# Regrouping the weight loads and moving the x transposes in a fused attention and maxout kernel on one Trainium2 core

## The chip, the core and the metric

The kernel runs on one core of a Trainium2 chip. Its engines are TensorE (PE, matmuls and transposes by matmul), VectorE (DVE), ScalarE (ACT), GpSimd (POOL) and SyncE (SP, which here only issues DMAs). The metric is the time of one execution on the device in microseconds (us); lower is better. Times of a kernel are given as the median of several runs. A single further execution is profiled, and all durations of rows come from that one.

## The reference

There are two stages. The first is a small attention in both directions between x (batch 8, heads 8, 512 positions, 64 wide) and 32 state vectors for each batch and head; the second is a feed-forward layer that takes the largest of three products.

```python
def _attn_ref(x, state):
    scale = 1.0 / np.sqrt(D)
    a  = softmax(scale * x @ state.T)          # per batch and head: 512 x 32
    xread = a @ state
    a2 = softmax(scale * state @ x.T)          # 32 x 512
    sread = a2 @ x
    return np.concatenate([xread, sread], axis=2)

def _moe_ref(x, w1, w2, w3, w_out):            # x: 4352 x 512, w: 512 x 768
    h = np.maximum(np.maximum(x @ w1, x @ w2), x @ w3)
    return h @ w_out                           # 768 x 512
```

The rows of the second stage are, for each batch, 512 rows of `xread` and 32 of `sread`, the heads side by side. (Softmax is written short here; the reference subtracts the maximum and divides by the sum.)

## The kernel before

The kernel is one program written out in program order under a manual schedule: every engine runs its instructions in the order in which the Python code emits them, and semaphores hold an instruction until its inputs and its buffer are there. Buffers come from pools that hand out a fixed number per tag in rotation, so an instruction that takes a buffer also waits until the last reader of that buffer's earlier tile has finished. In PSUM there are four buffers of tag `pw`[...] and two of tag `two`.

`xread` is never formed. Since `xread` is `a @ state` and the layer multiplies it by W, the kernel multiplies the states of a batch with W first (`g_cols`, giving G) and then a with G (`x_maxout`). W has 768 columns in six slices of 128, numbered m = 0 to 5; slice m of w1, w2 and w3 is needed together. For one batch b the steps are:

- `x_transpose(b, g, copy)`, on PE, or `x_transpose_dma(b)`, a DMA transpose issued by SP: x of the batch to `xT`. Batches 0, 1 and 2 use PE, 3 to 7 the DMA.
- `scores(b, g0, g1)`: PE multiplies `xT` with a block-diagonal arrangement of the states (`bd`; one tile `bds[k]` serves batches 2k and 2k+1), ACT takes the exponential to `e`.
- `softmax(b, g0, g1, mul)`: DVE sums and inverts, and `mul` (POOL or DVE) writes the product a.
- `a_transpose(b, g, copy)` on PE, or `a_transpose_dma(b)` by SP: a to `aT`.
- `g_cols(b, ms, copies, defer)`: eight small matmuls for each slice m of `ms`, then a copy of the slice of G out of PSUM by the engine named (ACT unless told otherwise), put off into the next maxout where `defer` says so.
- `x_maxout(b, m)`: six matmuls, ACT copies the first product (`t0`), DVE takes the two maxima and writes `ht`.
- `ffn_out(b, j)`: six matmuls of `ht` with `wout_sb`, a copy by ACT, and after every second j a store by POOL.
- `sread(b)`: the other direction, 32 small matmuls, two DVE instructions, and a DMA transpose by SP into `ats`, which is put on a list and issued by `late_transposes`.

`states(k, copy)` makes `bds[k]`: for k = 0 and 1 with PE transposes, for k = 2 and 3 with a DMA transpose by SP into `stT` and two POOL copies.

All loads that change the type from float32 to bfloat16 (W, x, w_out) are issued by POOL, in program order with POOL's own arithmetic. `load_x(b)` brings one batch of x, `load_st(k, eng)` the states of two batches, `load_w(c, parts)` one chunk of W by three DMAs. The chunks are slices 0, 1, 2-3 and 4-5. Half of x of batch 0 is loaded by SP in float32 and cast by DVE, so that the start doesn't wait for POOL. `keep_busy(n)` runs n matmuls on zeros whose result nobody reads.

The code has three parts: the loads and preparations; the start, written out by hand (from the first `keep_busy(5)`, line 329, to the loop), where the attention of batches 0, 1 and 2 is laid between the first slices of maxout; and the main loop over b = 2 to 7. In the loop each `x_maxout(b, m)` is followed by the list `slots[m]`, which holds the attention of batch n = b + 1, the missing slices of G, and `ffn_out(b - 1, j)`. The order within a slot is that in which the lists were filled.

Of the kernel before, what the change touches and what calls it, by code (L numbers as in the profile page):

```python
# [15 lines left out]
def kernel(  # L16
# [14 lines left out]
    nc = tc.nc  # L31

    B, H, S, D = x.shape
# [11 lines left out]
    XW = H * J * D  # L45
# [11 lines left out]
    def load_st(k, eng):  # L57
        eng.dma_start(
            out=st_f[k],
            in_=state[2 * k:2 * k + 2].rearrange("b h n d -> (b h n) d").rearrange("(p t) d -> p t d", t=4))  # L60
# [8 lines left out]
    def load_x(b):  # L69
        nc.gpsimd.dma_start(  # L70
            out=x_sb[b][:, 0:XW].rearrange("p (h jd) -> p h jd", h=H),
            in_=x[b].rearrange("h (p j) d -> p h (j d)", j=J))
# [9 lines left out]
    ident = const.tile([128, 128], BF16, name="ident")  # L82
    make_identity(nc, ident)
    nc.gpsimd.dma_start(out=x0_sb[1], in_=x0_heads(1))
    load_x(1)

    chunks = ((0, 1), (1, 2), (2, 4), (4, 6))
    w_sb = [wpool.tile([128, HS, 3, (m1 - m0) * 128], BF16, name=f"w{m0}") for m0, m1 in chunks]
    wout_sb = wpool.tile([128, NM, d_model], BF16, name="wout")

    def load_w(c, parts=(0, 1, 2)):
        m0, m1 = chunks[c]
        for i in parts:
            w = (moe_w1, moe_w2, moe_w3)[i]
            nc.gpsimd.dma_start(  # L95
                out=w_sb[c][:, :, i, :],
                in_=w.rearrange("(kk p) f -> p kk f", p=128)[:, :, m0 * 128:m1 * 128])
# [4 lines left out]
        return w_sb[c], slice(f, f + 128)  # L102

    load_w(0)
    for b in range(B):
        nc.gpsimd.memset(x_sb[b][:, XW:XW + D], 1.0)
    load_w(1, (0,))
    bds = [data.tile([128, 2, H, 2, Ns], BF16, name=f"bd{k}") for k in range(B // 2)]
    nc.vector.memset(bds[0], 0.0)

# [4 lines left out]
    def keep_busy(n):  # L115
        p = pp.tile([128, 1024], F32, tag="two", name="idle")
        for _ in range(n):
            nc.tensor.matmul(p[:, 0:512], zero[:, 0:128], zero, start=True, stop=True)  # L118
# [7 lines left out]
    def states_cast(k, cast):  # L126
        cast(out=st[k], in_=st_f[k].unsqueeze(2).to_broadcast((128, 4, 2, D)))
# [16 lines left out]
    xT, e, a, aT, G, ht, osb = {}, {}, {}, {}, {}, {}, {}  # L144

    def new(d, b, shape, name, bufs=2):
        d[b] = work.tile(shape, BF16, tag=name, bufs=bufs, name=name)

    def x_transpose(b, g, copy):

        if g == 0:
            new(xT, b, [128, H, 2, 128], "xT")
        p = pp.tile([128, HS, 2, 128], BF16, tag="pw", bufs=4, name="pxt")
        for s in range(HS):
            for jj in range(2):
                nc.tensor.transpose(
                    p[:, s, jj, :],
                    xv[b][:, 2 * s + g, 2 * jj:2 * jj + 2, :].rearrange("p j d -> p (j d)"), ident)
        copy(out=xT[b].rearrange("p (s g) j t -> p g s j t", g=2)[:, g], in_=p)  # L159

    def x_transpose_dma(b):
        new(xT, b, [128, H, 2, 128], "xT")
        nc.sync.dma_start_transpose(out=xT[b].rearrange("p h j t -> p (h j) t"), in_=x_sb[b][:, 0:XW])

    def scores(b, g0, g1):
        n = g1 - g0
        if g0 == 0:
            new(e, b, [128, J, 2, HS, Ns], "e")
        if n == 2:
            p = pp.tile([128, J, n, HS, Ns], F32, tag="two", name="ps")  # L170
        else:
            p = pp.tile([128, J, n, HS, Ns], F32, tag="pw", bufs=4, name="psh")
        for jj in range(2):
            for g in range(g0, g1):
                for s in range(HS):
                    h = 2 * s + g
                    nc.tensor.matmul(  # L177
                        p[:, 2 * jj:2 * jj + 2, g - g0, s, :], xT[b][:, h, jj, :],
                        bd(b, h).rearrange("p c n -> p (c n)"),
                        start=(g == g0 and s == 0 and (n == 2 or jj == 0)),  # L180
                        stop=(g == g1 - 1 and s == HS - 1), skip_group_check=True)
        nc.scalar.activation(out=e[b][:, :, g0:g1], in_=p, func=AF.Exp, scale=scale)  # L182

    def softmax(b, g0, g1, mul):
        n = g1 - g0
        if g0 == 0:
            new(a, b, [128, J, 2, HS, Ns], "a")
        den = work.tile([128, J, n, HS], F32, tag=f"den{n}", name="den")
        nc.vector.reduce_sum(out=den, in_=e[b][:, :, g0:g1], axis=AX.X)  # L189
        rden = work.tile([128, J, n, HS], F32, tag=f"rden{n}", name="rden")  # L190
        nc.vector.reciprocal(out=rden, in_=den)  # L191
        mul(  # L192
            out=a[b][:, :, g0:g1].rearrange("p j g s n -> p j (g s) n"),
            in0=e[b][:, :, g0:g1].rearrange("p j g s n -> p j (g s) n"),
            in1=rden.rearrange("p j g s -> p j (g s)").unsqueeze(3).to_broadcast((128, J, n * HS, Ns)))

    def a_transpose(b, g, copy):

        if g == 0:
            new(aT, b, [128, J, 2, 128], "aT", bufs=3)  # L200
        p = pp.tile([128, J, 128], BF16, tag="pw", bufs=4, name="pat")
        for j in range(J):
            nc.tensor.transpose(p[:, j, :], a[b][:, j, g].rearrange("p s n -> p (s n)"), ident)
        copy(out=aT[b][:, :, g, :], in_=p)
# [76 lines left out]
    def x_maxout(b, m):  # L281
        maxout(b, m, 512,
               lambda i, k: G[b][:, k, m * 384 + i * 128:m * 384 + i * 128 + 128],
               lambda k: aT[b][:, :, k, :], 2)
# [40 lines left out]
    def late_transposes():  # L325
        while late:
            late.pop(0)()
# [8 lines left out]
    x_transpose(0, 0, dve)  # L336
    x_transpose(0, 1, dve)
    scores(0, 0, 1)
    softmax(0, 0, 1, nc.gpsimd.tensor_mul)
    load_w(1, (1, 2))  # L340
    scores(0, 1, 2)
    softmax(0, 1, 2, nc.vector.tensor_mul)
    keep_busy(4)
    x_transpose(1, 0, act)
    x_transpose(1, 1, dve)
    a_transpose(0, 0, act)
    a_transpose(0, 1, dve)
    g_cols(0, (0,), (dve,))
    scores(1, 0, 1)
    scores(1, 1, 2)  # L350
    load_w(2)
    softmax(1, 0, 1, nc.gpsimd.tensor_mul)
    load_w(3, (0,))
    softmax(1, 1, 2, nc.gpsimd.tensor_mul)
    load_w(3, (1, 2))
    load_st(1, nc.gpsimd)
    load_x(2)
    x_maxout(0, 0)
    g_cols(0, (1,))
    g_cols(1, (0,))  # L360
    sread(0)
    x_maxout(0, 1)
    nc.gpsimd.dma_start(out=wout_sb, in_=moe_w_out.rearrange("(kk p) f -> p kk f", p=128))
    for k in range(2, B // 2):
        load_st(k, nc.gpsimd)
    load_x(3)
    sread(1)
    a_transpose(1, 0, act)
    a_transpose(1, 1, dve)
    g_cols(0, (2, 3), defer=(False, True))  # L370
    x_maxout(1, 0)
    x_maxout(0, 2)
    g_cols(1, (1, 2), defer=(False, True))
    x_maxout(0, 3)
    states_cast(1, pool)
    g_cols(0, (4, 5), defer=(False, True))
    x_maxout(1, 1)
    states(1, act)
    x_transpose(2, 0, dve)
    x_transpose(2, 1, act)  # L380
    x_maxout(0, 4)
    g_cols(1, (3, 4), defer=(False, True))
    x_maxout(1, 2)
    scores(2, 0, 2)
    x_maxout(0, 5)
    g_cols(1, (5,))
    x_maxout(1, 3)
    softmax(2, 0, 2, nc.gpsimd.tensor_mul)
    late_transposes()
    x_transpose_dma(3)  # L390
# [1 line left out]
    x_maxout(1, 4)  # L392
    g_cols(2, (0, 1))
    ffn_out(0, 1)
    load_x(4)
    for k in range(2, B // 2):
        states_cast(k, pool)
    x_maxout(1, 5)
# [3 lines left out]
    ffn_out(0, 2)  # L402
    ffn_out(0, 3)
    late_transposes()


    for b in range(2, B):
        n = b + 1
        slots = [[] for _ in range(NM)]
        if n < B:  # L410
            if n + 1 < B:
                slots[0].append(lambda: x_transpose_dma(n + 1))
            slots[0].append(lambda: scores(n, 0, 2))
            slots[1].append(lambda: softmax(n, 0, 2, nc.gpsimd.tensor_mul))
            slots[2].append(lambda: a_transpose_dma(n))
            if n % 2 and n + 1 < B:
                slots[2].append(lambda: states((n + 1) // 2, pool))
            slots[5].append(late_transposes)
            if n + 2 < B:
                slots[0].append(lambda: load_x(n + 2))  # L420
        else:
            for m in range(NM):
                slots[m].append(lambda m=m: s_maxout(m))
        slots[1].append(lambda: g_cols(b, (2, 3)))
        slots[2].append(lambda: g_cols(b, (4, 5)))
        if n < B:
            slots[3].append(lambda: sread(n))
            slots[4].append(lambda: g_cols(n, (0, 1), defer=(False, True)))
        for j, m in enumerate((1, 2, 4, 5)):
            slots[m].insert(0 if m > 2 else len(slots[m]), lambda j=j: ffn_out(b - 1, j))  # L430
        for m in range(NM):
            x_maxout(b, m)
            for f in slots[m]:
                f()
# [36 lines left out]
```

## Time and profile before

| what | value |
|---|---|
| median of 5 runs | 160.56 us (160.24 to 161.56) |
| the profiled execution, own time | 161.74 us |
| its span (first to last instruction) | 160.0 us |
| PE busy | 149.5 us (93%) |
| ACT busy, DVE busy, POOL busy | 96.8, 94.6, 51.0 us |
| DMA moved | 21.72 MB, mean 136 GB/s |
| DMA transposes of x: issue on SP, min, median, max | 1.33, 3.18, 6.46 us |
| DMA transposes of x: to landing, min, median, max | 4.3, 5.0, 9.1 us |
| DMA transposes of the states (`stT`): to landing | 2.5 and 3.5 us |

Times in the profile are microseconds from the start of the span. In the page's second part the span is cut into 40 equal slices of 4 us, and a digit is a busy share in tenths; PEclk is the clock that PE was granted, in tenths. A line of the chain of waits has the start, the length and the engine with its line number. A line of the timeline has start, length, engine, line, operation, the tile written and the tile read, and in brackets the idle time before and what ended it. A line of the waits has the total, the number and the longest. "PEq" and "SPq" are the sequencers of PE and SP; a DMA's row on SPq or POOL is the time of issuing it, not that of the transfer.

### The profile page before, as it was taken

Reading aid. Unit: us, or ns where it says so; the run is one execution under the profiler, and the core shown is the slowest. Engines: PE = TensorE matmul, PEld = TensorE weight load, DVE = VectorE, ACT = ScalarE, POOL = GpSimd, SP = SyncE. Lnnn points to the kernel's source line nnn. Section 1 sums busy time; section 2 is a strip of 40 time slices with the busy share of each in tenths; the row PEclk is TensorE's granted clock in tenths of the full one; section 3 lists DMA queues with packets and bytes.
Section 4 is the critical chain, followed back from the end, with each engine's and each line's share of the span. In section 5 each row is a group of like instructions: output and inputs, shape, how many; then the busy total and the mean of one; then the engine's idle time right before and its main releaser. Section 6 shows DMA issues by size and latency. Waiting matters only on the chain.

```text
span 160.0 us, 3568 instructions
## 1 busy us (share of the span) xinstructions
PE 149.5 (93%) x1432; PEld 70.7 (44%) x1432; DVE 94.6 (59%) x161; ACT 96.8 (61%) x156; POOL 51.0 (32%) x72
## 2 busy tenths in 40 slices
PE   6775799999999999999999999999999999999990
PEld 2442353544454444444444444444434465466550
DVE  4788358668545864577367736673767384475200
ACT  3364548995737837783778287828782737633340
POOL 8859981000553404541034061410051100100150
PEclk9999779999999999999999999999999999999999
DMA  3999999998079997999969967070307030030365
GB/s 117 207 164 119 189 195 177 234 135 133 0 159 242 137 141 130 277 165 170 201 171 118 101 124 280 4 205 2 135 0 205 0 137 0 0 131 4 131 220 173
DMA packets 36720, 21.72 MB, mean 136 GB/s; under 512 B 21952, under 2 KB 34368, under 8 KB 36704
## 3 DMA queue, kind: packets, MB, share of 16 engines
q0 software_dynamic: 17216, 15.08, 49.8%
q1 hardware_dynamic: 19344, 6.29, 23.0%
q8 instruction: 11, 0.18, 0.4%
q10 hardware_dynamic: 144, 0.13, 0.2%
q14 instruction: 5, 0.04, 0.1%
HBM read 15.20 MB, written 8.91 MB: 151 GB/s over the span
## 4 chain that ended last, share of the span: by engine, by line
PE 83%; DMA 6%; DVE 4%; ACT 3%; POOL 1%; issue 1%; SPq 0%; DVEq 0%; POOLq 0%
PE pw L271 42%; PE po L308 28%; PE pg L250 7%; DMA w<-in_moe_w_dram 3%; PE psr L222 3%; DMA x0f<-in_x_dram 2%; PE ps L177 2%; DVE t L278 1%; ACT t L275 1%; ACT G L256 1%; DVE ht L279 1%; PE ph L300 1%; POOL a L192 1%; DVE x L335 1%; POOL w L95 0%
## 5 line engine op out<-in xcount | busy, mean ns | idle before, releaser
L271 PE MATMUL pw<-aT,G 128*128 128x512 bf16 x288 | 71.3, 385 | 0.9 <-DVE G L256 0.5
L278 DVE TENSOR_TENSOR t<-t,pw 128x512 bf16<-128x512 bf16 (+1 forms) x54 | 35.1, 649 | 42.9 <-ACT t L275 27.1
L308 PE MATMUL po<-wout,ht 128*128 128x512 bf16 x198 | 47.4, 380 | 0.2 <-DVE ht L279 0.2
L256 ACT CAST G<-pg 128x768 bf16<-128x768 f32 x47 | 36.3, 806 | 8.3 <-PE pg L250 7.9
L271 PEld LDWEIGHTS <-G 128*128 128x128 bf16 x288 | 26.6, 98 | 33.0 <-issue 3.9
L279 DVE TENSOR_TENSOR ht<-t,pw 128x512 bf16<-128x512 bf16 (+1 forms) x54 | 35.5, 658 | 5.6
L275 ACT CAST t<-pw 128x512 bf16<-128x512 f32 (+1 forms) x54 | 30.6, 566 | 13.0 <-PE pw L271 12.3
L311 ACT COPY osb<-po 128x512 f32<-128x512 f32 x33 | 19.3, 586 | 23.6 <-PE po L308 23.2
L308 PEld LDWEIGHTS <-ht 128*128 128x128 bf16 x198 | 17.8, 98 | 24.7 <-issue 4.5
L192 POOL TENSOR_TENSOR a<-e,rden 128x1024 bf16<-128x1024 bf16 (+1 forms) x9 | 14.6, 1621 | 40.0 <-DVE rden L191 30.6
L320 POOL DMA_DIRECT2D out_dram<-osb x14 | 7.9, 566 | 46.5 <-ACT osb L311 36.7
L250 PE MATMUL pg<-w,bd 64*32 64x384 bf16 x384 | 12.8, 328 | 2.5 <-DMA w<-in_moe_w_dram 2.2
L189 DVE TENSOR_REDUCE den<-e 128x32 f32<-128x1024 bf16 (+1 forms) x10 | 9.9, 991 | 0.5 <-ACT e L182 0.5
L95 POOL DMA_DIRECT2D w<-in_moe_w_dram x12 | 9.1, 774 | 0.0
L250 PEld LDWEIGHTS <-bd 64*32 64x32 bf16 x384 | 3.6, 89 | 12.4 <-issue 11.8
L271 PE MATMUL pw<-ats,w 128*128 128x256 bf16 x72 | 8.8, 273 | 0.0
L182 ACT ACTIVATE e<-ps 128x1024 bf16<-128x1024 f32 x6 | 6.1, 1024 | 3.8 <-PE ps L177 3.7
L271 PEld LDWEIGHTS <-w 128*128 128x128 bf16 x72 | 7.1, 98 | 2.1
L140 POOL COPY bd<-stT 64x512 bf16<-64x512 bf16 x4 | 4.3, 1071 | 10.8 <-DMA stT<-st 10.7
L70 POOL DMA_DIRECT2D x<-in_x_dram x7 | 6.5, 923 | 0.0
L118 PE MATMUL idle<-zero 128*128 128x512 bf16 x14 | 4.9, 492 | 1.2 <-DVE zero L81 1.2
L177 PEld LDWEIGHTS <-xT 128*128 128x128 bf16 x128 | 4.7, 98 | 2.4 <-DVE xT L159 0.8
(45 smaller groups left out, 66.3 us busy)
## 6 DMA issues: line engine op xcount, KB each, us to landing
out_dram<-osb POOLq DMA_DIRECT2D x14, 512.0 KB, 3.7
x<-in_x_dram POOLq DMA_DIRECT2D x7, 512.0 KB, 9.2
w<-in_moe_w_dram POOLq DMA_DIRECT2D x6, 256.0 KB, 6.0
w<-in_moe_w_dram POOLq DMA_DIRECT2D x6, 128.0 KB, 6.8
wout<-in_moe_w_out_dram POOLq DMA_DIRECT2D x1, 768.0 KB, 11.7
x0f<-in_x_dram SPq DMA_DIRECT2D x1, 512.0 KB, 4.0
out_dram<-osb SPq DMA_DIRECT2D x1, 512.0 KB, 2.7
stf<-in_state_dram POOLq DMA_DIRECT2D x3, 128.0 KB, 11.0
```

Of the source, the lines that this page charges most:

```text
L95: nc.gpsimd.dma_start(out=w_sb[c][:, :, i, :], in_=w.rearrange("(kk p) f -> p kk f", p=128)[:, :, m0 * 128:m1 * 128])
L177: nc.tensor.matmul(p[:, 2 * jj:2 * jj + 2, g - g0, s, :], xT[b][:, h, jj, :], bd(b, h).rearrange("p c n -> p (c n)"), start=(g == g0 and s ...
L189: nc.vector.reduce_sum(out=den, in_=e[b][:, :, g0:g1], axis=AX.X)
L192: mul(out=a[b][:, :, g0:g1].rearrange("p j g s n -> p j (g s) n"), in0=e[b][:, :, g0:g1].rearrange("p j g s n -> p j (g s) n"), in1=rden.r ...
L250: nc.tensor.matmul(p[32 * s:32 * s + 32, g, 0:384].rearrange("p (i f) -> p i f", i=3), bd(b, 2 * s + g)[64 * g:64 * g + 64, g, :], w[64 * ...
L256: copy(out=G[b][:, :, m * 384:(m + 1) * 384], in_=p[:, :, 0:384])
L271: nc.tensor.matmul(p[:, 0:n], lhs(i, k), rhs(k), start=(k == 0), stop=(k == nk - 1))
L275: nc.scalar.copy(out=t0[:, 0:n], in_=pw[0][:, 0:n])
L278: nc.vector.tensor_max(t1[:, 0:n], t0[:, 0:n], pw[1][:, 0:n])
L279: nc.vector.tensor_max(ht[b][:, m, :], t1[:, 0:n], pw[2][:, 0:n])
L308: nc.tensor.matmul(p, ht[b][:, m, j * 128:(j + 1) * 128], wout_sb[:, m, :], start=(m == 0), stop=(m == NM - 1))
L311: act(out=o[:, j, :], in_=p)
```

## The change

- W is cut into three chunks of two slices each instead of four (1, 1, 2, 2). `load_w` always loads all three matrices of a chunk. The first chunk is issued ahead of x of batch 1, the second ahead of batch 0's first product on POOL, the third behind it.
- The start is reordered: slices of `g_cols` and `x_maxout` of batch 0 come ahead of and between the steps of batch 1's attention. Some copies go to other engines (`g_cols(0, (1,))` and slice 3 to DVE, the second `a_transpose(1, ...)` to ACT). `sread(0)` and `sread(1)` come later.
- Of the eight memsets that write the column of ones behind x, two stay at the top and six move behind the loads.
- x is loaded one batch further ahead (`load_x(4)` in the start, then `n + 3` in the loop).
- `xT` gets three buffers instead of two. The DMA transpose of batch n + 2 is issued in slot 2, behind that of a(n), where before that of batch n + 1 was issued in slot 0; that of batch 4 is issued ahead of the loop.

```diff
-    load_x(1)
-
-    chunks = ((0, 1), (1, 2), (2, 4), (4, 6))
+
+    chunks = ((0, 2), (2, 4), (4, 6))
...
-    def load_w(c, parts=(0, 1, 2)):
+    def load_w(c):
         m0, m1 = chunks[c]
-        for i in parts:
-            w = (moe_w1, moe_w2, moe_w3)[i]
+        for i, w in enumerate((moe_w1, moe_w2, moe_w3)):
...
     load_w(0)
-    for b in range(B):
+    load_x(1)
+    for b in range(2):
         nc.gpsimd.memset(x_sb[b][:, XW:XW + D], 1.0)
-    load_w(1, (0,))
...
-            new(xT, b, [128, H, 2, 128], "xT")
+            new(xT, b, [128, H, 2, 128], "xT", bufs=3)
...
     def x_transpose_dma(b):
-        new(xT, b, [128, H, 2, 128], "xT")
+        new(xT, b, [128, H, 2, 128], "xT", bufs=3)
...
     scores(0, 0, 1)
+    load_w(1)
     softmax(0, 0, 1, nc.gpsimd.tensor_mul)
-    load_w(1, (1, 2))
     scores(0, 1, 2)
     softmax(0, 1, 2, nc.vector.tensor_mul)
-    keep_busy(4)
+    keep_busy(5)
+    g_cols(0, (0,))
+    a_transpose(0, 0, act)
+    a_transpose(0, 1, dve)
+    g_cols(0, (1,), (dve,))
+    load_w(2)
+    load_st(1, nc.gpsimd)
+    x_maxout(0, 0)
     x_transpose(1, 0, act)
     x_transpose(1, 1, dve)
-    a_transpose(0, 0, act)
-    a_transpose(0, 1, dve)
-    g_cols(0, (0,), (dve,))
+    x_maxout(0, 1)
     scores(1, 0, 1)
     scores(1, 1, 2)
-    load_w(2)
     softmax(1, 0, 1, nc.gpsimd.tensor_mul)
-    load_w(3, (0,))
     softmax(1, 1, 2, nc.gpsimd.tensor_mul)
-    load_w(3, (1, 2))
-    load_st(1, nc.gpsimd)
     load_x(2)
-    x_maxout(0, 0)
-    g_cols(0, (1,))
-    g_cols(1, (0,))
-    sread(0)
-    x_maxout(0, 1)
     nc.gpsimd.dma_start(out=wout_sb, in_=moe_w_out.rearrange("(kk p) f -> p kk f", p=128))
     for k in range(2, B // 2):
         load_st(k, nc.gpsimd)
     load_x(3)
-    sread(1)
+    load_x(4)
+    for b in range(2, B):
+        nc.gpsimd.memset(x_sb[b][:, XW:XW + D], 1.0)
+    g_cols(0, (2, 3), (act, dve))
+    sread(0)
+    g_cols(1, (0,))
+    x_maxout(0, 2)
     a_transpose(1, 0, act)
-    a_transpose(1, 1, dve)
-    g_cols(0, (2, 3), defer=(False, True))
+    a_transpose(1, 1, act)
+    g_cols(1, (1,))
+    x_maxout(0, 3)
     x_maxout(1, 0)
-    x_maxout(0, 2)
-    g_cols(1, (1, 2), defer=(False, True))
-    x_maxout(0, 3)
-    states_cast(1, pool)
     g_cols(0, (4, 5), defer=(False, True))
     x_maxout(1, 1)
+    states_cast(1, pool)
+    x_maxout(0, 4)
+    sread(1)
+    g_cols(1, (2, 3), defer=(False, True))
+    x_maxout(0, 5)
     states(1, act)
     x_transpose(2, 0, dve)
     x_transpose(2, 1, act)
-    x_maxout(0, 4)
-    g_cols(1, (3, 4), defer=(False, True))
     x_maxout(1, 2)
+    g_cols(1, (4, 5), defer=(False, True))
+    x_maxout(1, 3)
     scores(2, 0, 2)
-    x_maxout(0, 5)
-    g_cols(1, (5,))
-    x_maxout(1, 3)
     softmax(2, 0, 2, nc.gpsimd.tensor_mul)
     late_transposes()
     x_transpose_dma(3)
...
-    load_x(4)
+    load_x(5)
...
     late_transposes()
+    x_transpose_dma(4)
...
         if n < B:
-            if n + 1 < B:
-                slots[0].append(lambda: x_transpose_dma(n + 1))
             slots[0].append(lambda: scores(n, 0, 2))
             slots[1].append(lambda: softmax(n, 0, 2, nc.gpsimd.tensor_mul))
             slots[2].append(lambda: a_transpose_dma(n))
+            if n + 2 < B:
+                slots[2].append(lambda: x_transpose_dma(n + 2))
             if n % 2 and n + 1 < B:
                 slots[2].append(lambda: states((n + 1) // 2, pool))
             slots[5].append(late_transposes)
-            if n + 2 < B:
-                slots[0].append(lambda: load_x(n + 2))
+            if n + 3 < B:
+                slots[0].append(lambda: load_x(n + 3))
```

## The prediction

> **What bounds the kernel now.** I read the page's part 2 first, because it tells which stretch of the span has room at all.
>
> ```profile
> PE   6775799999999999999999999999999999999990
> ...
> PEclk9999779999999999999999999999999999999999
> ```
>
> TensorE is full from the sixth slice (4 us each) to the end; only the first five slices, 0 to 20 us, have gaps, and slices five and six ran at a reduced clock. The waits of PE and the chain that ended last say which gap it is.
>
> ```profile
> PE pg L250 <- DMA w<-in_moe_w_dram: 2.2, 2, 1.7
> ```
>
> ```profile
> 10.76 0.75 POOL w L95
> 11.51 5.27 DMA w<-in_moe_w_dram
> 16.77 0.14 issue
> 16.91 0.40 PE pg L250 x8
> ...
> 18.18 2.73 PE pw L271 x6
> 20.92 0.92 PE psr L222 x32
> ...
> 38.00 1.46 PE po L308 x6
> ```
>
> The second slice of W is issued by POOL only after the softmax product that ends at 10.76, lands at 16.8, and PE starts on it at 16.91 after 1.74 us of waiting. The next line to see is 18.18: six matmuls take 2.73 us where the same six take 1.29 later in the chain. At 38.00 the first output projection starts; from there the chain is PE almost without a break, so what is won or lost before 38 us goes straight into the end. Up to there the kernel before and the changed one do the same list: ten `x_maxout`, twelve `g_cols` slices, the attention of batches 0 and 1, x and scores of batch 2. I therefore compare the time at which `ffn_out(0, 0)` starts.
>
> Behind 38 us what can hurt is a new wait of PE. The timeline of the main loop shows the tightest cover.
>
> ```profile
> 51.47 6.46 SPq L163 DMA_TRANSPOSE xT<-x  x1
> ...
> 54.35 1.91 POOL L192 TENSOR_TENSOR a<-e,rden 128x1024 bf16<-128x1024 bf16 x1 [4.16 <-DVE rden L191]
> ...
> 58.02 1.45 SPq L208 DMA_TRANSPOSE aT<-a  x1
> ...
> 59.52 1.26 SPq L137 DMA_TRANSPOSE stT<-st  x1
> ...
> 62.06 2.21 POOL L140 COPY bd<-stT 64x512 bf16<-64x512 bf16 x2 [5.80 <-DMA stT<-st]
> ...
> 64.70 0.63 PE L177 MATMUL ps<-bd,xT 128*128 128x64 bf16 x16
> ```
>
> The block-diagonal states of batch 4 (`bd`) are finished by POOL at 64.27, and the scores of batch 4 read them on PE at 64.70: 0.43 us of slack. The same pair for batch 6 is 94.92 and 96.22: 1.30 us.
>
> [...]the granted clock is 0.50 from 18.25 to about 21.6, 3.4 us, after a stretch (14.8 to 18.2) with about 1.5 us of PE work. [...]the x transpose of 51.47 landed after 9.1 us (60.6), and the two short ones behind it landed right after it, at 61.5 and 62.05. [...]a slice of W gives bf16 runs of 256 B, two give 512 B. Here one-slice pieces landed 0.75 us apart per 131 KB (175 GB/s) and two-slice pieces 1.35 us apart per 262 KB (194 GB/s), so this is worth little.
>
> **The change, part by part. Loads.** POOL's queue before: half of x0, x1, slice 0 of W, slice 1, slices 2-3, 4-5. After: half of x0, slices 0-1 (three issues of 0.77 us), x1, slices 2-3 and, behind the first product, 4-5. All of chunk 1 is then issued by about 8.5 us, so the queue no longer runs dry behind the product of 9.71 (the DMA moved 84 to 146 GB/s from 12 to 15 us, 172 to 201 when full). Landings, from bytes: up to 6.36 us, when the half of x0 lands, 1.01 MB had moved, 0.655 of them by SP, so 0.36 MB of POOL's queue. x0 and slices 0-1 are 1.05 MB: the remaining 0.69 at 0.18 MB/us take 3.8 us, to 10.2. In the trace a piece lands 1.2 us after its bytes are counted (slice 0: counted 11.0, landed 12.2), so slices 0-1 are there at **11.4**, x1 (0.52 MB) at 14.3, slices 2-3 (0.79 MB at 0.19) at 18.4; about 0.6 us of doubt each. Three of x, 2, 3 and 4, still follow with wout; x3 lands at about 34 and x4 at 37, and the transposes that read them are not needed before 47. Six of eight memsets move behind the loads: 0.1 us each, POOL is idle there.
>
> **Start, step by step.** Scores of batch 0 end at 8.5 as now; five idle matmuls instead of four (0.22 us) lie inside a wait. `g_cols(0, 0)` waits to 11.4 (now 12.26), PE to 11.65; ACT copies G 0.80 us and then aT 0.59, so `x_maxout(0, 0)` starts at 13.1 instead of 13.70. x of batch 1 has landed when the maxout's 1.3 us are over; eight transposes, `x_maxout(0, 1)` and the scores of batch 1 fill PE to about 17.3, with waits for `pw` buffers (four, freed by ACT and DVE). The kernel before has the same work behind it only after 20.9. Then PE waits for slices 2-3 to 18.4, 1.1 us. From there DVE sets the pace: its queue from the end of `x_maxout(0, 1)`, 18.1, holds the softmax of batch 1 (4 pieces, 1.9 us), one G copy of 0.96 (now DVE's, as is slice 1's; aT of batch 1 goes to ACT, 0.59), two `sread` (0.5 each), one xT copy 0.68 and eight maxouts of 1.40: 15.7 us, to 33.8 if it never waits. It waits for ACT, whose two aT copies and a G copy stand ahead of the t0 of `x_maxout(0, 3)` (1.7 us) and whose xT copy stands ahead of that of `x_maxout(1, 2)` (1 us). So `ffn_out(0, 0)` comes at **36.6**, 1.4 us earlier.
>
> From that I take off 0.6: between 8.0 and 11.4 PE has about 0.4 us of scores and 1.1 of idle matmuls, as little as in the stretch that was followed by half clock. A stretch of 3.4 us at half clock from 11.4 would double some 1.4 us of transposes and maxout; part lies under ACT's copies. Ends: nothing, and the 1.8 us that it cost before. Start: **-0.8** (from -2.0 to +1.0).
>
> **Transposes of x.** None of PE's waits is for an xT by DMA: that of batch 5 lands at 68.5 and is read at 80.46. Moving it ahead and a third xT buffer gain nothing by themselves. But its place matters on SP's queue. Before, the x transpose is issued in slot 0, ahead of the wait for the product a. After, in slot 2, between aT(n) and, for odd n, the transpose of the states (rows 7 to 10 of SP's order: aT, xT, stT, ats). Then stT comes behind 512 KB. From the end of the product a(3), time zero: aT 1.3 us of issue, xT 3.2 (median of five; 1.33 to 6.46), stT to landing 3.0 (2.5 and 3.5), two POOL copies 2.2 and a few hundredths: 9.75 us. The cover is 64.70 - 56.26 = 8.44 us. For n = 5 it is 96.22 - 87.84 = 8.38. So PE would wait 1.3 us at the scores of batch 4 and 1.4 at those of batch 6. [...]Above: 6.46 gives over 4 each. The x loads are a batch earlier, so both transposes meet little traffic; I take 1.0 each, **+2.0** (0 to +6). Behind PE at that point stands everything; behind POOL's copies stand the stores of batch n - 2 and a load of x, with over 10 us to spare. Late ats are read only at the end. The transposes of batches 3 and 4 meet x loads earlier than now, under 10 us of cover: nothing.
>
> **Sum:** -0.8 + 2.0 = +1.2. The profiled span of 160.0 (own time 161.74, 1.18 above the median) becomes 161.2; the median of 160.56 becomes **161.8**.
>
> **The rivals.** (1) *The start decides.* If the three transposes run at the pace of batch 7's, the states are in time[...], and with PE kept at full clock the 1.4 to 2.0 us stay: 160.56 - 1.4 = 159.2. For it: 0.43 and 1.30 us of slack exist already and traffic is lighter. Against: four of the five x transposes took 2.9 us or more to issue. It decides when stT is issued within about 3.2 us of the product's end. (2) *They cancel*: 1.4 won, 0.7 lost twice, 160.6. (3) *Half clock at the start and full waits*: nothing won at the start, 1.3 us lost twice, 163.1; a wait of 2 us at batch 4 could bring half clock there too. (4) *Nothing happens* because loads are bound by bytes alone: contradicted by the 84 to 146 GB/s around 13 us; it would give 160.6 and is counted with 2.
>
> **How the numbers follow.** About 0.5% (0.8 us) is what a measurement here can tell from no change. Forecast 0.40 (161.4 to 162.5, all slower), rival 3 0.15, rivals 2 and 4 0.25, rival 1 0.20: faster 0.20, same 0.25, slower 0.55. The range takes in rivals 1 and 3 and half of the bounds: 159.2 to 163.5; the forecast's own is 161.2 to 162.6.
>
> **What would show it.** Right: `pg` waits for `w` near 11.4 and again near 18.4, `ffn_out(0, 0)` between 36 and 38, and new waits "PE ps <- POOL bd" at the scores of batches 4 and 6, with stT issued more than 4 us after the product. Wrong: those waits missing (then rival 1), half clock after 11.4 (rival 3), or `ffn_out(0, 0)` later than 38.5, because ACT or POOL, not the loads, hold the start.

## The result, and the profile after

The changed kernel takes 1.0065 times as long as the kernel before, 95% interval 1.0042 to 1.0088: about 1.05 us slower on the 161.29 us that 79 runs of the kernel before have as median. (The ratios leave out executions more than 1.5% above the fastest of their kernel: 26 of the changed kernel's 44, which run from 160.8 to 171.8 us with a median of 164.74, so that 1.0065 speaks of its faster 18; 16 of the 22 of `e10` below; and the ones profiled for `e3`, `e4` and `e10`.) The profiled execution has a span of 160.9 us, 0.9 above before, and an own time of 162.72. In the sources of the new profiles the line numbers of functions are two lower: `x_maxout`'s matmuls are L269, `ffn_out`'s L306, `g_cols` L248, scores L175, the copies of `bd` L138.

Part 2 of the page, PE's busy share and granted clock in slices of 4 us:

```profile
PE   7849889999999998999999988999999999999990
...
PEclk9995999999999999999999999999999999999999
```

The half clock is still there, now in the fourth slice (12 to 16 us) instead of the fifth and sixth, and there are new dents in PE's row in the 16th and 24th and 25th slices, at 64 and 96 us. PE's waits (total, number, longest) name them:

```profile
PE pg L248 <- DMA w<-in_moe_w_dram: 2.0, 1, 2.0
PE ps L175 <- POOL bd L138: 1.8, 2, 1.3
```

The chain that ended last, at the start:

```profile
3.86 7.60 DMA w<-in_moe_w_dram
11.46 0.14 issue
11.60 0.40 PE pg L248 x8
...
13.36 2.64 PE pw L269 x6
```

The first chunk of W is there at 11.46, and the first six matmuls of maxout again take 2.64 us, now right behind the wait, at a granted clock of 0.50 from 12.5 to 15.5 us. The timeline of batch 3's attention and of batch 5's, in order on SP, POOL and PE:

```profile
36.81 1.46 PE L306 MATMUL po<-wout,ht 128*128 128x512 bf16 x6
...
46.02 4.86 SPq L161 DMA_TRANSPOSE xT<-x  x1
...
53.16 1.91 POOL L190 TENSOR_TENSOR a<-e,rden 128x1024 bf16<-128x1024 bf16 x1 [4.16 <-DVE rden L189]
...
55.09 1.24 SPq L206 DMA_TRANSPOSE aT<-a  x1
...
56.51 2.82 SPq L161 DMA_TRANSPOSE xT<-x  x1
...
59.38 1.26 SPq L135 DMA_TRANSPOSE stT<-st  x1
...
61.90 2.19 POOL L138 COPY bd<-stT 64x512 bf16<-64x512 bf16 x2 [6.84 <-DMA stT<-st]
...
64.14 0.63 PE L175 MATMUL ps<-bd,xT 128*128 128x64 bf16 x16 [0.46 <-POOL bd L138]
...
88.64 3.62 SPq L161 DMA_TRANSPOSE xT<-x  x1
92.31 1.26 SPq L135 DMA_TRANSPOSE stT<-st  x1
...
94.89 2.17 POOL L138 COPY bd<-stT 64x512 bf16<-64x512 bf16 x2 [7.62 <-DMA stT<-st]
...
97.11 0.63 PE L175 MATMUL ps<-bd,xT 128*128 128x64 bf16 x16 [1.29 <-POOL bd L138]
```

`ffn_out(0, 0)` starts at 36.81 instead of 38.00: the start has won 1.19 us. At the scores of batch 4 PE waits 0.46 us for `bd`, at those of batch 6 1.29, and the copies of `bd` wait for stT, which is issued behind the x transpose. The scores of batch 4 are 0.56 us earlier than before (64.14 against 64.70), those of batch 6 are 0.89 later (97.11 against 96.22), and that is the difference of the spans. In the kernel before, the scores of batch 6 had no wait:

```profile
96.22 0.63 PE L177 MATMUL ps<-bd,xT 128*128 128x64 bf16 x16
```

### The profile page after: what moved, and what is told of

Its sections match the earlier page's. It is cut to its first block, busy times and chain, and to the rows that moved or that the text cites. A ratio compares the mean times of both kernels' runs of the same rounds, so it can differ in the third digit from the quotient of the medians.

```text
span 160.9 us, 3570 instructions
## 1 busy us (share of the span) xinstructions
PE 149.9 (93%) x1433; PEld 71.0 (44%) x1433; DVE 94.9 (59%) x161; ACT 96.6 (60%) x156; POOL 48.7 (30%) x69
## 4 chain that ended last, share of the span: by engine, by line
PE 70%; issue 7%; POOL 7%; DMA 6%; ACT 3%; DVE 3%; SPq 1%; POOLq 0%; DVEq 0%
PE pw L269 36%; PE po L306 23%; PE pg L248 5%; DMA w<-in_moe_w_dram 5%; POOL bd L138 3%; POOL a L190 2%; PE psr L220 2%; PE ps L175 2%; ACT t L273 2%; DMA stT<-st 2%; DVE t L276 1%; SPq L161 1%; POOL w L93 1%; DVE ht L277 1%; PE ph L298 1%
## 5 line engine op out<-in xcount | busy, mean ns | idle before, releaser
L269 PE MATMUL pw<-aT,G 128*128 128x512 bf16 x288 | 71.2, 384 | 0.6 <-ACT aT L202 0.4
L306 PE MATMUL po<-wout,ht 128*128 128x512 bf16 x198 | 47.4, 380 | 0.0
L254 ACT CAST G<-pg 128x768 bf16<-128x768 f32 x46 | 35.8, 807 | 10.6 <-PE pg L248 10.2
L269 PEld LDWEIGHTS <-G 128*128 128x128 bf16 x288 | 26.7, 98 | 33.2 <-issue 4.9
L306 PEld LDWEIGHTS <-ht 128*128 128x128 bf16 x198 | 17.8, 98 | 24.1 <-issue 4.0
L318 POOL DMA_DIRECT2D out_dram<-osb x14 | 8.0, 570 | 45.2 <-ACT osb L309 36.6
L248 PE MATMUL pg<-w,bd 64*32 64x384 bf16 x384 | 13.0, 331 | 2.6 <-DMA w<-in_moe_w_dram 2.0
L269 PE MATMUL pw<-ats,w 128*128 128x256 bf16 x72 | 8.8, 273 | 0.0
L248 PEld LDWEIGHTS <-bd 64*32 64x32 bf16 x384 | 3.6, 89 | 11.6 <-issue 10.7
L138 POOL COPY bd<-stT 64x512 bf16<-64x512 bf16 x4 | 4.2, 1059 | 14.6 <-DMA stT<-st 14.5
L269 PEld LDWEIGHTS <-w 128*128 128x128 bf16 x72 | 7.0, 98 | 2.1
L175 PEld LDWEIGHTS <-xT 128*128 128x128 bf16 x128 | 4.8, 98 | 4.6 <-issue 2.3
L93 POOL DMA_DIRECT2D w<-in_moe_w_dram x9 | 6.8, 768 | 0.0
L116 PE MATMUL idle<-zero 128*128 128x512 bf16 x15 | 5.6, 527 | 1.2 <-DVE zero L81 1.2
```

The lines of the kernel that those rows point to most:

```text
L93: nc.gpsimd.dma_start(out=w_sb[c][:, :, i, :], in_=w.rearrange("(kk p) f -> p kk f", p=128)[:, :, m0 * 128:m1 * 128])
L138: copy(out=bds[k][r, :, :, c, :].rearrange("p b h (q t) -> p (b h) q t", t=4), in_=p[r].rearrange("p t (k q) -> p k q t", q=8))
L248: nc.tensor.matmul(p[32 * s:32 * s + 32, g, 0:384].rearrange("p (i f) -> p i f", i=3), bd(b, 2 * s + g)[64 * g:64 * g + 64, g, :], w[64 * ...
L254: copy(out=G[b][:, :, m * 384:(m + 1) * 384], in_=p[:, :, 0:384])
L269: nc.tensor.matmul(p[:, 0:n], lhs(i, k), rhs(k), start=(k == 0), stop=(k == nk - 1))
L306: nc.tensor.matmul(p, ht[b][:, m, j * 128:(j + 1) * 128], wout_sb[:, m, :], start=(m == 0), stop=(m == NM - 1))
```

## The experiments

Theory: the change is two changes with opposite signs. The new start gains because the first chunk of W lands early; the loop loses because stT comes behind the x transpose of batch n + 2. Rivals: the waits on `bd` come from traffic (loads of x one batch earlier, the shifted start) and not from the order on SP; and the start gains by its order of steps, not by the order of loads.

**Each half alone, and one swap.** `e2_start_only` takes the start without the loop, `e3_loop_only` the loop without the start, `e1_states_first` swaps two lines of the changed kernel:

```diff
             slots[2].append(lambda: a_transpose_dma(n))
-            if n + 2 < B:
-                slots[2].append(lambda: x_transpose_dma(n + 2))
             if n % 2 and n + 1 < B:
                 slots[2].append(lambda: states((n + 1) // 2, pool))
+            if n + 2 < B:
+                slots[2].append(lambda: x_transpose_dma(n + 2))
```

> The changed kernel with one swap in slot 2 of the loop: the DMA transpose of the states (stT) is issued on SP ahead of the x transpose of batch n + 2, not behind it. If the new waits of PE at the scores of batches 4 and 6 (0.46 and 1.29 us in the changed kernel's trace) come from that place in SP's queue, both vanish, POOL's copies of bd start about 3 us earlier, and the time falls by about 1.7 us against the changed kernel, to some 0.7% below the kernel before. Rival: the copies are late because POOL or the DMA rings are busy with loads and stores there; then stT still lands late, the waits stay above 0.5 us in sum, and the time stays within 0.5 us of the changed kernel.

> Only the first half of the change: three chunks of W and the new order of the start; the loop, the two xT buffers and the loads of x in it are as before. If start and loop add up independently, ffn_out(0, 0) starts at 36.8 us as in the changed kernel (38.0 before) and PE has no wait at the scores of batches 4 and 6: about 1.1 us faster than before, ratio 0.993. Rival: the third xT buffer and the earlier loads of x are needed for the start; then ffn_out(0, 0) comes later than 37.5 and the ratio is 1.00.

> Only the second half of the change: x transposes two batches ahead in slot 2, three xT buffers, x loaded one batch further ahead; W's chunks and the order of the start are as before. If the waits on bd belong to the loop alone, PE waits 0.4 to 0.6 us at the scores of batch 4 and 1.2 to 1.4 at those of batch 6, and the time is 1.6 to 2.0 us above before, ratio 1.010 to 1.012. Rival: in the changed kernel they came from the shifted start, which left x loads to collide with the transposes; then the waits are under 0.5 us in sum and the ratio is about 1.00.

Measured: e1 0.9928 (0.9900 to 0.9957), e2 0.9925 (0.9898 to 0.9953), e3 1.0097 (1.0040 to 1.0154). The halves add up: 0.9925 times 1.0097 is 1.0021, and the change itself 1.0065, within their intervals. In e3's profile the waits are there with the old start, at both places and 0.6 us longer in sum than the 2.0 I had expected at most; e2 has none in its list. The line is of PE's waits in e3:

```profile
PE ps L177 <- POOL bd L140: 2.6, 2, 1.5
```

The swap of e1 takes away the wait at batch 6 altogether and moves that copy of `bd` to 91.65, but not the wait at batch 4, where I had expected none. Its timeline:

```profile
45.81 5.19 SPq L161 DMA_TRANSPOSE xT<-x  x1
...
54.89 1.25 SPq L206 DMA_TRANSPOSE aT<-a  x1
56.19 1.27 SPq L135 DMA_TRANSPOSE stT<-st  x1
...
61.67 2.18 POOL L138 COPY bd<-stT 64x512 bf16<-64x512 bf16 x2 [6.81 <-DMA stT<-st]
...
63.90 0.63 PE L175 MATMUL ps<-bd,xT 128*128 128x64 bf16 x16 [0.43 <-POOL bd L138]
```

stT is issued 3.2 us earlier than in the changed kernel (56.19 against 59.38) and lands at almost the same time (61.6 against 61.9). The trace's DMA issues (the last number is the time from issue to landing) point to the reason:

```profile
x<-in_x_dram POOLq DMA_DIRECT2D x1, 512.0 KB, 12.3
xT<-x SPq DMA_TRANSPOSE x1, 12.6
```

The x transpose of batch 4, issued ahead of the loop at 45.81, lands only at 58.4, beside the load of x of batch 6, issued at 47.89. aT and stT stand behind it in SP's queue and land at 61.1 and 61.6. In the changed kernel's profile, whose code is the same up to the issue of aT, the transpose took 9.9 us and landed at 55.9, 0.8 us after the issue of aT (55.09); there it can have delayed stT, which landed 2.5 us after its own issue, by little.

**The load beside that transpose.** `e6_load_later` moves one line of e1; `e10_after_load_later` does the same to the changed kernel, where stT stays behind the x transpose.

```diff
-                slots[0].append(lambda: load_x(n + 3))
+                slots[3].append(lambda: load_x(n + 3))
```

> The kernel of e1 with one move: load_x(n + 3) from slot 0 to slot 3 of the loop, so that x of batch 6 is loaded after the transposes of batch 3's attention and not beside the x transpose of batch 4. In e1 that transpose, issued at 45.8 us, landed only at 58.4, and stT behind it in SP's queue at 61.6. If the load beside it makes it late, it lands near 54, stT of batch 4 by about 59, and the rest of the wait at the scores of batch 4 (0.43 us in e1, 2.40 in e4) is gone; ratio 0.985 to 0.991, and less spread. Rival: the output store and the load of x of batch 5 alone make it late; then it lands after 57 and the ratio stays at 0.993.

> The changed kernel with load_x(n + 3) moved from slot 0 to slot 3 only; stT stays behind the x transpose. If both the place in SP's queue and the load beside the transpose of batch 4 feed the waits on bd, the wait at batch 4 stays at 0.3 to 0.8 us and that at batch 6 at about 1.3 (no x load is near it in either kernel): 1.6 to 2.1 us in sum, ratio 1.000 to 1.005, with runs closer together than those of the changed kernel. Rival: the load alone makes them; then both are under 0.3 us and the ratio equals e6's 0.989.

Measured: e6 0.9887 (0.9844 to 0.9929), no wait on `bd`. The timeline of e6:

```profile
44.65 5.10 SPq L161 DMA_TRANSPOSE xT<-x  x1
...
55.05 1.26 SPq L135 DMA_TRANSPOSE stT<-st  x1
...
57.64 2.20 POOL L138 COPY bd<-stT 64x512 bf16<-64x512 bf16 x2 [3.93 <-DMA stT<-st]
...
62.15 0.63 PE L175 MATMUL ps<-bd,xT 128*128 128x64 bf16 x16
```

The x transpose of batch 4 landed at 55.8, 11.1 us after its issue and later than the 54 I had expected, but before aT (57.0); stT landed 2.5 us after its issue, and `bd` is finished 2.3 us before the scores. That the load is what made the transpose late in e1 is likely, but not shown: with the load beside it the transpose took 9.9 us in the changed kernel, 12.6 in e1, 13.8 in e3 and 12.5 in e4, without it 11.1 in e6, 9.1 in e10 and 9.0 in e9, and the intervals of e1 and e6 overlap. e10 gives 1.0000 (0.9956 to 1.0043). Its waits:

```profile
PE ps L175 <- POOL bd L138: 3.1, 2, 2.1
```

Here the transpose of batch 4 had landed at 53.7, so on SP nothing stood in the way but the x transpose of batch 5, landed at 59.5, and stT behind it at 62.1. Between e10 and e6 only the two lines of the swap differ: 1.0000 against 0.9887. By these ratios the order on SP is the larger part (1.1% from e10 to e6, 1.4% from the changed kernel to e1) and the load the smaller (0.65% from the changed kernel to e10, 0.4% from e1 to e6), and only the larger part is clear of the intervals. My expected range for the waits' sum (1.6 to 2.1) was too low for this profile: the wait at batch 4 is 2.09 us. PE came to it sooner, since `ffn_out(0, 0)` is at 35.39 here and not at 36.81, and stT took 5.1 us to land; why it did, the trace doesn't say. The runs do lie closer together, from 160.1 to 166.3 us.

**The order of the loads.** `e8_x1_first` is e2 with x of batch 1 ahead of the first chunk:

```diff
-    load_w(0)
     load_x(1)
+    load_w(0)
```

> The kernel of e2 with load_x(1) ahead of load_w(0), as in the kernel before, everything else of the new start kept. If POOL's queue is bound by bytes, the first chunk lands about 2.9 us later, at 14.3 instead of 11.4, PE waits that much longer, and ffn_out(0, 0) comes 2 to 3 us later than in e2; ratio 1.005 to 1.012. Rival: the order of the first two loads matters little, since x of batch 1, with its transposes, is needed right behind them and the same bytes must land before the second slices; then ffn_out(0, 0) comes within 0.7 us of e2 and the ratio is below 0.998.

Measured: 1.0161 (1.0114 to 1.0208). The wait in its list, and the first output projection:

```profile
PE pg L248 <- DMA w<-in_moe_w_dram: 5.4, 1, 5.4
```

```profile
40.36 1.46 PE L306 MATMUL po<-wout,ht 128*128 128x512 bf16 x5
```

PE's wait ends at 14.99 instead of 11.43, and `ffn_out(0, 0)` comes 4.7 us later than in e2 (35.69), more than the 3.6 of the landing: the mean clock of the span is 0.979, with a reduced clock in two slices, 12 to 20 us. The ratio is above the 1.012 that I had expected at most. Without W first the new order of the start is a loss. The size of the chunks and the place of the memsets were not tested apart.

**Filling PE's wait for W.** Three kernels try to win back the half clock. `e4_fill_wait` is e1, `e5_start_fill` is e2 with more idle matmuls; `e7_at_first` is e2 with other work in the wait:

```diff
-    keep_busy(5)
+    keep_busy(14)
```

```diff
-    keep_busy(5)
-    g_cols(0, (0,))
+    keep_busy(10)
     a_transpose(0, 0, act)
     a_transpose(0, 1, dve)
+    g_cols(0, (0,))
```

> The kernel of e1 with 14 instead of 5 idle matmuls ahead of the first g_cols, so that PE works through its wait for the first chunk of W (8.3 to 11.4 us). If the half clock from about 12.2 to 15.6 us comes from that idle stretch, it vanishes: the first maxout takes 1.3 instead of 2.64 us, and ffn_out(0, 0) starts 0.5 to 1.0 us earlier than in e1; the time falls by as much. Rival: the half clock doesn't come from this stretch, or its cost lies under the copies and x of batch 1 anyway; then ffn_out(0, 0) comes within 0.2 us of e1.

> The kernel of e2 (new start, loop as before) with 14 instead of 5 idle matmuls ahead of the first g_cols. If the half clock behind PE's wait for the first chunk of W costs the start about 1.1 us (ffn_out(0, 0) at 36.6 to 36.8 with it, at 35.7 in the profile of e2 without it) and comes in about half of the runs of e2, the mean falls by some 0.5 us, ratio about 0.989, and the runs lie closer together. Rival: the fill buys nothing, because the half clock then comes elsewhere or a later landing sets the pace, as in e4; the ratio stays at 0.9925 or is higher.

> The kernel of e2 with the transposes of a of batch 0 ahead of the first g_cols on PE, which waits for W, and 10 idle matmuls ahead of them. The aT copies then lie inside the wait, and x_maxout(0, 0) can start when slice 0 of G is copied, at about 12.7 us instead of 13.2 (e2). If PE's early order is on the path, ffn_out(0, 0) comes about 0.4 us earlier than in e2 without half clock (35.3), and ratio is about 0.988. Rival: the second chunk of W at 18.0 to 18.9 us or x of batch 1 at 14.1 sets the pace behind it; then ffn_out(0, 0) stays at 35.6 or later and the ratio at 0.990 to 0.993.

Measured: e4 0.9965 (0.9934 to 0.9997), e5 0.9949 (0.9923 to 0.9975), e7 0.9915 (0.9890 to 0.9939). No half clock is at the start of these three profiles, nor of e9's below: the six matmuls of the first maxout take 1.45 to 1.47 us. But of the six profiles with the new start and no more idle matmuls, those of e2, e6 and e10 have none either (1.46 each), and only those of the changed kernel, e1 and e8 do (2.64, 2.72 and 2.63). The ratios of e4 and e5 are not below those of e1 and e2, and that of e7 can't be told from e2's. In the profiles something else sets the pace each time: in e4 the second chunk of W, for which PE waits until 19.01, and a wait of 2.40 us on `bd`; in e5 the cast of x of batch 0, 0.4 us late; in e7 the first chunk itself, which lands only at 12.6. Landings of one and the same load lie 1 to 2 us apart between profiles (in e1 and e7 10.8 and 12.6 for the first chunk, 17.7 and 19.4 for the second), which is as much as the fill could bring. That the half clock costs is seen in e2, whose profile happened to be without one, with the same start as the changed kernel's:

```profile
13.19 1.46 PE L269 MATMUL pw<-aT,G 128*128 128x512 bf16 x6 [0.56 <-ACT aT L202]
...
35.69 1.46 PE L306 MATMUL po<-wout,ht 128*128 128x512 bf16 x5
```

The first maxout takes 1.46 us on this view instead of 2.64, and `ffn_out(0, 0)` comes at 35.69 instead of 36.81: 1.1 us, of which the first chunk, 0.17 us earlier here, accounts for a little. So neither that the fill cures the clock nor that it brings time is shown, and neither is refuted.

**The best of both.** `e9_both` has the loop of e6 and the start of e7.

> The loop of e6 (states first, x loaded in slot 3) with the start of e7 (transposes of a ahead of the first g_cols, 10 idle matmuls). If the two gains are independent, e6's 0.9887 falls by what e7 won on e2 (0.001 to 0.004): ratio 0.985 to 0.988, no wait of PE on bd, no half clock at the start. Rival: the second chunk of W sets the start in any order, and the ratio stays within 0.002 of e6.

Measured: 0.9888 (0.9860 to 0.9917), the same as e6, as the rival said. PE has no wait on `bd`. e6, the changed kernel with two edits in the loop, has the lowest ratio, 1.1% below the kernel before and 1.8% below the changed one; e1, e2, e7 and e9 beat both kernels too, and their intervals overlap that of e6.

## Why the prediction was right

The forecast was +1.2 us, from -0.8 at the start and +2.0 in the loop; the runs give +1.05, the profile +0.9 from -1.19 at the start, +1.75 of waits and +0.33 that came with the waits (last section). The path was right: the start gains, and the copies of `bd` wait for stT, which is issued behind the x transpose, 4.3 and 5.0 us after the end of the product. That the loop came to 2.08 where 2.0 was forecast is luck: one wait was half as long as taken, the other longer, and the 0.33 wasn't in the sum.

- **Loads.** First chunk 11.4, measured 11.46; x of batch 1 14.3, measured 14.1 (issued at 4.59, 9.5 us to landing). PE did not reach the second chunk before 18.59, so the predicted wait at 18.4 did not show in the changed kernel; in e2, with full clock, PE waited until 18.07. Counting bytes from the windows plus the 1.2 us of tail read in the trace of before held to 0.4 us in these two profiles; in others the first chunk landed as early as 10.8 (e1) and as late as 12.6 (e7), so 0.6 us of doubt was too little. e8, at 1.0161, shows that without W first the start doesn't gain.
- **The start.** Two terms were mis-sized and partly cancelled. The schedule gave 36.6 at full clock (its parts add up to 36.5) where e2 shows 35.69. DVE's queue was priced well: in e2 its list ends at 36.70, with 2.9 us of waits for ACT where 2.7 were taken. What failed is the step from there to `ffn_out(0, 0)`, which was put at the end of DVE's list. In e2 PE starts it at 35.69, 1.0 us before the end of DVE's last instruction for the maxouts ahead of it:

```profile
36.01 0.69 DVE L277 TENSOR_TENSOR ht<-t,pw 128x512 bf16<-128x512 bf16 x1
```

  That maximum is of batch 1, and `ffn_out(0, 0)` reads only `ht` of batch 0. The half clock was charged with 0.6 us and cost about 1.1. The sum of -0.8 was 0.4 short of the -1.19 measured. That PE would fall to half clock behind a stretch with 1.5 us of work was right for this execution; in e2's profile the same stretch (PE busy 1.50 us from 8.0 to 11.5, and 1.49 in the changed kernel) was followed by full clock, granted 1.00 from 11.5 to 15.5. So PE's busy time in that stretch does not by itself tell whether half clock follows; what decides it was not shown.
- **The wait at batch 6.** 1.0 taken, 1.29 measured. By the prediction's medians the sum was 1.4; the reduction to 1.0, for lighter traffic, was not earned. The x transpose, with no load of x beside it, took 3.62 us to issue, stT landed 2.5 after its issue, the copies took 2.2.
- **The wait at batch 4.** 1.0 taken, 0.46 measured. In the changed kernel's profile the named path accounts for it: from the end of the product a(3) (55.07) 1.44 us to the issue of the x transpose, 2.87 to that of stT, 2.52 to the copies and 2.24 to the scores are 9.07, against a cover of 8.61; the x transpose (2.82 for 3.2) and stT (2.5 for 3.0) were priced too high. But there is a second cause, which the prediction put at nothing: "The transposes of batches 3 and 4 meet x loads earlier than now, under 10 us of cover: nothing." In e1, e3 and e4 the transpose of batch 4 landed 12.5 to 13.8 us after its issue and stT behind it, so that e1 and e4, with stT issued first, still wait 0.43 and 2.40. Nor was it true that the earlier x loads leave both x transposes in little traffic: that of batch 5 was issued at 56.51, and the load of x of batch 6 landed at 57.8.
- **Transposes further ahead gain nothing.** So it was: e2, with transposes one batch ahead and two buffers, and e1 have the same ratio, and no profile has a wait of PE on an xT made by DMA.
- **The rivals.** Rival 1, faster by the start alone, is what e1 and e2 show, where no x transpose comes between aT and stT; in the changed kernel's profile it was excluded by x transposes that took 2.8 and 3.6 us to issue, not 1.3. Rival 3 came half true: half clock at the start, but with a gain left over.

## What to carry to other kernels

When a transfer is moved on a queue whose transfers land in the order of issue, as the transposes issued by SP did wherever their landings were read (in e1 those issued at 45.81, 54.89 and 56.19 us landed at 58.4, 61.1 and 61.6, in the changed kernel those issued at 55.09, 56.51 and 59.38 at 58.8, 60.9 and 61.9), list what is issued behind it and look for the one with the least slack; here two small transposes of states with 0.4 and 1.3 us of slack turned a gain of 0.75% into a loss of 0.65%, and swapping two lines gave it back. Issuing something two steps ahead is not free when nothing waited for it: here it stood ahead of a transfer that did have a reader. Load first what the first full-rate work of the bound engine needs (e2 with W first 0.9925, e8 with x of batch 1 first 1.0161); put a price on it by bytes in the queue plus the tail (0.18 MB/us and 1.2 us here), and allow for the 1.8 us by which the landing of the first chunk differed between profiles here.

## What was not expected of the hardware

- The same DMA transpose of x (512 KB, batch 4) landed 8.2 to 13.8 us after its issue in these profiles; 9.9 and 12.6 are from the changed kernel and e1, whose code is the same up to the issue of aT. That of batch 3, issued ahead of the loop's loads, took 4.6 to 5.1 in the kernel before, the changed one, e1 and e4.
- A wait of PE of a little over 2 us in the middle of dense work was followed by half clock in two profiles: in e10 after a wait of 2.09 us that ended at 64 us, in e4 after one of 2.40 us that ended at 66 us (granted 0.50 from 67 to 69). The windows of e10 (columns: stretch, length, busy time of PE, PE's weight loads, DVE, ACT and POOL, then the granted clock, DMA share and GB/s):

```profile
65.00:66.00 1.00, 1.00 (x4) 0.36 (x3) 0.00 (x0) 0.93 (x2) 1.00 (x2) 0.64 0.62 246
66.00:67.00 1.00, 1.00 (x3) 0.15 (x1) 0.40 (x1) 0.57 (x2) 0.29 (x1) 0.50 0.79 279
67.00:68.00 1.00, 1.00 (x18) 0.28 (x18) 0.90 (x3) 0.37 (x1) 0.00 (x0) 0.50 0.75 50
```

  The waits of 0.46 and 1.29 us in the changed kernel's profile and of 1.51 us in e3's had no such sequel: the granted clock was 1.00 from 64.8 to 69 and from 97 to 101 us in the changed kernel, and in e3 the scores of batch 5 come 15.76 us behind those of batch 4 (82.89 and 67.13), as in the kernel before. So a wait on `bd` can cost more than itself, as these two did; how often that happened in the changed kernel's runs was not measured.
- Each of the two waits moved the scores behind it by about 0.15 us more than its own length (0.46 and 1.29 in the waits, 0.17 and 0.16 more in the start times of the scores of batches 4 and 6, counted from `ffn_out(0, 0)` and from batch 4's scores).
